# First layer of the first tile by halves of the contraction, with tiny matmuls ahead, in a fused attention and ReGLU kernel

## The chip, the cores and the metric

The kernel runs on one core of a Trainium2 chip. The metric is the device time of one execution in microseconds, taken as the median of several runs; smaller is better. The core has a matrix engine (TensorE, written PE, whose weight loads are listed apart as PEld), a vector engine (VectorE, DVE), a scalar engine (ScalarE, ACT), GpSimd (POOL) and SyncE (SP). Each works through its own queue of instructions in order and waits where a semaphore tells it to. Matmuls write to PSUM, which has eight banks here. POOL and SP also issue DMA transfers.

## The reference

```python
scores = scale * np.matmul(q, k.transpose(0, 1, 3, 2))      # q, k, v: 8 x 8 x 576 x 64
mask = (rel >= 0) & (rel < 64)                              # causal, a window of 64
attn = softmax(np.where(mask, scores, -1e9))
x = np.matmul(attn, v).transpose(0, 2, 1, 3).reshape(4608, 512)
out = (np.maximum(x @ w_gate, 0.0) * (x @ w_val)) @ w_out   # 512 -> 1536 -> 512
```

Inputs and the output are 32-bit floats; the kernel computes in 16-bit floats with 32-bit sums.

## The kernel before, in words

**Two parts in one stream.** Attention is cut into units of 192 query rows (`U`), all eight heads: three units for each of the eight batches. The layers behind it work on tiles of tokens: four tiles of 384 (`TT`, two units each), then six of 512. Tiles 0 and 1 run the plain layers `hidden` and `output`; later tiles run a form with fewer products (`fast_hidden`, matmuls on L634), and the last ones one with seven products for the second layer (`SevenOut`, `SevenLast`, matmuls on L847, with an order of products by name in the table `SEVEN`).

**Who does what.** For a unit: `qk_load` brings q or k of one half of the heads on POOL's DMA queue into `nats` (L179), `qk_trans` transposes it on DVE (L199), `u_st` computes scores on PE (L265, 48 matmuls), `u_exp` takes exponentials on ACT (L299), `u_mask` multiplies by the band on DVE (L306), `u_pv` multiplies by v on PE (L336, 48 matmuls for each half of the heads), `u_recip` (L350) and `u_norm` (L357) normalise on DVE, `u_turn` (L379) transposes into the tile `xt`. v arrives by `v_load` (POOL's queue, L205) and is copied to other partitions by `v_spread`, by DMAs on SP's queue (L217) or, where a copying engine is named, by that engine (L215). `behind_masks` (L312) puts tiny copies on POOL behind a unit's masks. Weight sums (L528) on POOL and DVE prepare the later tiles.

**First layer.** For each of 12 blocks of 128 columns (`f`), `hidden` multiplies the tile by `wg` into one bank and by `wv` into another, four matmuls each over the contraction of 512 (`c` = 0 to 3). ACT applies the ReLU to the first (L572), DVE multiplies it with the second (the gate, L575). In tile 0 the blocks go in pieces of four; the first piece goes by units, in spans of 192 tokens with two blocks in a bank. The weights come in three pieces of 512 columns for each of `wg` and `wv` (`G3`, `V3`), each piece in two DMAs by halves of the contraction (`w_load`, L159), so `c` = 0, 1 can land before `c` = 2, 3. `output` (L1023) is the second layer: out of `g_sb`, with `wo`; ACT copies a bank out (L1035), SP stores it (L1036).

**Banks.** Banks 0 to 3 go round by `one_bank`, banks 4 to 7 in pairs by `two_banks` (scores and pv).

**What sets the order.** The kernel writes all engines' queues in one pass. An object `W` keeps a planned clock. The first and second layers write their matmuls in a fixed order and move the clock by their planned length; every other step has a planned time (`W.at(time, step)`) and is written where the clock passes it. `w_need` moves the clock to the planned landing of a weight piece. The planned times only decide the order in which instructions stand in their queues; in the run each waits only for its data and its place. `plan_batch` gives the planned times of a batch's four q and k loads and of its four transposes; `pair(t, TA, TB, P)` plans the scores of a tile's two units at `TA` and `TB`, and pv, norms and turns from `P` on.

**The start.** PE begins with `u_bias`: eight matmuls (L232) write the band's bias into all banks. `keep_hot` (L229) and `heat` (L226) are matmuls on zeros with no use for the result.

Of the kernel before, what the change touches and what calls it, by code (L numbers as in the profile page):

```python
# [47 lines left out]
def kernel(  # L48
# [10 lines left out]
    nc = tc.nc  # L59
# [4 lines left out]
    U = 192  # L64
    UB = S // U
    NU = B * UB
    NC = DM // 128
    NF = DF // 128
# [85 lines left out]
    def w_load(wt, src, f0, f1, landed):  # L154

        if wt is not wo:
            ns = slice(128 * f0, 128 * f1)
            for a in range(2):
                nc.gpsimd.dma_start(wt[:, 2 * a:2 * a + 2, ns], src.rearrange("(a p e) n -> a p e n", a=2, e=2)[a, :, :, ns])  # L159
        if wt is wo:  # L160
            nc.gpsimd.dma_start(wo[:, f0:f1], src.rearrange("(c p) n -> p c n", p=128)[:, f0:f1])
        w_done.update(((wt.name, f), landed) for f in range(f0, f1))

    def w_need(wt, f):
        while (wt.name, f) not in w_done:
            W.pop()
        W.advance(w_done[wt.name, f])

# [17 lines left out]
    def first_round(name, copies):  # L188
        n = S // 32 * D // len(copies)
        to = nat[0, name, 0] = nats[:, 2 * "kq".index(name)]  # L190
        for i, copy in enumerate(copies):
            copy(to[:, n * i:n * i + n], nat["32", name][:, n * i:n * i + n])
# [30 lines left out]
    def heat(n, to, start=True):  # L223

        for _ in range(n):
            nc.tensor.matmul(to, zero[:, 0:128], zero[:, 0:to.shape[1]], start=start, stop=start, skip_group_check=not start)  # L226

    def keep_hot(to):
        nc.tensor.matmul(to, zero32[:, 0:128], zero32[:, 0:to.shape[1]], start=False, stop=False, skip_group_check=True)  # L229
# [6 lines left out]
    def one_bank():  # L236
        taken["one"] += 1
        to = singles[(taken["one"] - 1) % 4]
        while id(to) in unread:
            W.pop()  # L240
        return to
# [41 lines left out]
    def u_st(u, hhs=(0, 1)):  # L283
        d = units.setdefault(u, {})
        if "st" not in d:
            st_tiles(u)
        run_rows([[st_block(d["st"][g][:, U * hh + 64 * w:U * hh + 64 * w + 64], g, hh, UB * u + w, "biased" in d)
                   for hh in hhs for w in range(UB)] for g in range(G)])
        return 0.29 * len(hhs)
# [117 lines left out]
    def part_written(banks):  # L407
        written.update((id(to), 0) for to in banks)
# [135 lines left out]
    def plan_values(T, u):  # L544
        W.at(T, lambda: u_pv(u))
        W.at(T + 0.6, lambda: u_recip(u))
        for hh in range(2):
            W.at(T + 0.8 + 0.5 * hh, lambda hh=hh: u_norm(u, hh))
        W.at(T + 1.8, lambda: u_turn(u))
# [4 lines left out]
        while normed[0] < n:  # L554
            W.pop()

    def hidden(t, spans, f0=0, f1=NF, each=1):

        if t not in gs:
            gs[t] = g_sb_p.tile([128, NF, WT], FP16, name="g_sb"), {}  # L560
        g_sb, done = gs[t]
        xt = xt_tile(t)
        n = spans[0][1] - spans[0][0]

        w = 512 // n
        each = max(each, w)

        def part(tile):
            return tile[:, 0:w * n].rearrange("p (w n) -> p w n", w=w)

        def relu(r_sb, h1):
            nc.scalar.activation(part(r_sb), part(h1), ACT.Relu)  # L572

        def gate(f, c0, r_sb, h2):
            nc.vector.tensor_tensor(g_sb[:, f:f + w, c0:c0 + n], part(r_sb), part(h2), MUL)  # L575
            done.update(dict.fromkeys(range(f, f + w), c0 + n))

        for fb in range(f0, f1, each):
            r2s = [f_sb.tile([128, 2, WT], FP32, name="pr", bufs=4) for _ in range(2)]
            r_sbs = {}  # L580
            for i, wt in enumerate((wg, wv)):
                for c0, f in ((c0, f) for c0, _ in spans for f in range(fb, fb + each, w)):
                    h = one_bank()
                    part_written([h])
                    for b in range(w):
                        W.advance(W.clock)
                        w_need(wt, f + b)
                        for c in range(NC):
                            nc.tensor.matmul(h[:, b * n:b * n + n], wt[:, c, (f + b) * 128:(f + b) * 128 + 128],  # L589
                                             xt[:, c, c0:c0 + n], start=(c == 0), stop=(c == NC - 1))  # L590
                        W.clock += 4 * (n + 7) / 2400.0
                    if i == 0:
                        r_sb = r_sbs[c0, f] = r2s[len(r_sbs) // 2][:, len(r_sbs) % 2]
                        W.at(W.clock, lambda r_sb=r_sb, h=h: relu(r_sb, h))
                    else:
                        W.at(W.clock, lambda f=f, c0=c0, r_sb=r_sbs[c0, f], h=h: gate(f, c0, r_sb, h))

    def fast_hidden(t, seven=None):

# [467 lines left out]
    XAT = -0.3  # L1067
    SEVEN_LAST = (("P6", "P5", "P2", "P7", "oP1", "P3", "P4"), ("P6", "P5", "P2", "P7", "oP1", "P4", "P3"))
    SEVEN = {n: ("P2", "v0", "v1", "P6", "P5a", "P7", "s0", "P5b", "P4", "s1", "P3") for n in (-5, -4, -3, -2)}
    SEVEN[-1] = ("v0", "P2", "P6", "v1", "P5a", "P7", "P5b", "P4", "h1", "P3")  # L1070

    SEVEN[0] = ("P2", "P4", "P5", "P6", "P7", "P3")

    with tc.manual_schedule():
# [21 lines left out]
        k_zeros()  # L1096
        band_bias()

        first_round("k", (dve, act))
        u_bias(0)  # L1100
        u_bias(1)
# [28 lines left out]
        u_norm(1, 0)  # L1130
        for hh in range(2):
            u_turn(1, (hh,))
        w_load(*G3[1], 20.3)
        w_load(*V3[1], 22.8)
        v_load(2)
        w_load(*G3[2], 27.0)
        w_load(*V3[2], 29.6)
        W.at(23.2, lambda: u_st(2))
        plan_exps(23.2, 2)
        plan_values(27.4, 2)  # L1140

        v_spread(2, pool)
        for name in "kq":
            for hh in range(2):
                qk_load(1, name, hh)
# [3 lines left out]
        for u in (4, 5):  # L1149
            v_load(u)  # L1150
        for i, (name, hh) in enumerate((n, hh) for n in "kq" for hh in range(2)):
            W.at(31.6 + 1.4 * i, lambda name=name, hh=hh: qk_trans(1, name, hh))
        for hh, T in enumerate((36.6, 38.8)):
            W.at(T, lambda hh=hh: u_st(3, (hh,)))
            for i in range(G):
                W.at(T + 0.4 + 0.22 * i, lambda hh=hh, i=i: u_exp(3, i, (hh,)))
                W.at(T + 0.8 + 0.22 * i, lambda hh=hh, i=i: u_mask(3, i, (hh,)))
            W.at(T + 3.5 - 0.7 * hh, lambda hh=hh: u_pv(3, (hh,)))
            W.at(T + 4.0 - 0.7 * hh, lambda hh=hh: u_recip(3, (hh,)))
            W.at(T + 4.1 - 0.7 * hh, lambda hh=hh: u_norm(3, hh))  # L1160
            W.at(T + 4.6 - 0.7 * hh, lambda hh=hh: u_turn(3, (hh,)))
        W.at(37.4, lambda: v_spread(3, pool))
        W.at(40.6, lambda: behind_masks(3))

        def pair(t, TA, TB, P):
            for u, T in ((2 * t, TA), (2 * t + 1, TB)):
# [10 lines left out]
            W.at(T + 1.9, lambda: u_turn(u))  # L1177
            return took

        plan_batch(2, (36.5, 36.6, 42.5, 42.6), (52.0, 53.6, 56.9, 57.1))  # L1180
        plan_batch(3, 58.0, None)
        W.at(58.0, lambda: v_load(8))
        for u in (6, 7):
# [1 line left out]
            W.at(58.0, lambda u=u: v_spread(u))  # L1185
        for u in (4, 5):
            W.at(45.6, lambda u=u: v_spread(u))
        pair(2, 46.6, 50.0, 54.0)
        W.at(52.7, lambda: behind_masks(5))
        pair(3, 62.6, 65.3, None)  # L1190
        W.at(68.0, lambda: behind_masks(7))
# [28 lines left out]
        def ahead(t):  # L1220
            T = W.clock
            long = widths[t] == WT
            ends = T + (32.7 if long else 22.5)
            if t + 2 <= LAST:
                qk_turns(t + 2, T, LATE if t - 1 in FAST_OUT else (0.1, 1.4, 8.0, 14.2) if long else (0.1, 1.4, 6.1, 10.7) if t < NS - 1 else (2.4, 6.1, 10.7, 14.2))
                v_ahead(t + 2, ends, ends + VAT if t in FAST_OUT else ends - 5.0 if long else T + 3.0 if t == 2 else ends + 1.5)
                if t + 1 == NS:
                    W.at(ends + 1.4, lambda: behind_quad(3))
            if t == NS - 2:
                W.at(ends - 0.9, lambda: behind_quad(0, 0))  # L1230
            if t + 3 <= LAST:
                qk_loads(t + 3, (ends - 0.89, ends - 0.88, ends - 0.87, ends - 0.86) if t == NS - 2 else (ends - 15.0, ends - 14.9, ends - 3.0, ends - 2.9) if t < NS else ends - QAT)

        sums = {w: [(w, j, n) for j in range(NF // 4) for n in (0, 1, 3, 2)] for w in (0, 1)}
        for T, gap, eng, some in ((40.5, 0.1, nc.gpsimd, sums[0][:4] + sums[1][:3]), (52.8, 0.1, nc.gpsimd, sums[1][3:8]),
                                  (48.2, 0.6, nc.vector, sums[0][4:8]), (68.1, 0.1, nc.gpsimd, sums[0][8:]),
                                  (64.5, 0.7, nc.vector, sums[1][8:])):
            for i, (w, j, n) in enumerate(some):
                W.at(T + gap * i, lambda eng=eng, w=w, j=j, n=n: w_form(eng, (wg, wv)[w], n, j))
# [9 lines left out]
                pass  # L1249

        W.advance(15.3)
        hidden(0, ((0, U), (U, TT)), 0, 4, 4)
        hidden(0, ((0, TT),), 4, NF, 4)
        hidden(1, ((0, U),), each=4)
        output(0, (0, 1), (0, 8, NF))
        ready(1)
        hidden(1, ((U, TT),), each=4)
        output(0, (2,))
        output(1)
        W.advance(W.clock)  # L1260
        while any(id(one) in unread for one in singles[:4]):
# [73 lines left out]
```

## Time and profile before

| | |
|---|---|
| median of three runs | 301.92 us (301.90 to 302.04) |
| profiled execution | 302.04 us |
| its span, first to last instruction | 300.3 us |
| granted TensorE clock, mean | 1.000 |
| PE busy | 289.6 us, 96% |
| DVE busy | 251.7 us, 84% |
| POOL busy | 201.7 us, 67% |
| ACT busy | 196.0 us, 65% |
| DMA moved | 33.20 MB, mean 111 GB/s |

The profile is one execution, recorded by the hardware. Busy shares are averages over the span; what a wait costs has to be read at its place. In a row of a timeline the first number is the start in us from the span's start, the second the length of the group, then engine, line, operation, output<-input, size, count, and in brackets the idle time before it with what ended it. Landings of loads are told by the time from issue to landing.

### The profile page before, as it was taken

The numbers are of one execution on the slowest core, as the hardware profiler recorded it, in microseconds if no ns is written. First come the engines' busy times: TensorE is split into PE (matmuls) and PEld (weight loads), VectorE is DVE, ScalarE is ACT, GpSimd is POOL, SyncE is SP. The second block draws the span as 40 slices with busy tenths as digits, with TensorE's granted clock in tenths as the row PEclk, the third lists the DMA queues.
The fourth block names the chain that finished last, engine by engine and source line by source line (L and its number), as shares of the span: only waits on it lengthen the run. The fifth ranks groups of instructions, "written<-read, shape, count | busy, mean of one in ns | idle before, by whom it ended". The sixth has DMA issues, their size and how long they took to land.

```text
span 300.3 us, 11073 instructions
## 1 busy us (share of the span) xinstructions
PE 289.6 (96%) x4643; PEld 239.4 (80%) x4643; DVE 251.7 (84%) x517; ACT 196.0 (65%) x408; POOL 201.7 (67%) x241
## 2 busy tenths in 40 slices
PE   4899999999999999999999999999999999999994
PEld 2475877748957975888888888888888888888894
DVE  5947895997995999789999899989858985896584
ACT  3545336258848848885798579857985698538850
POOL 8767689868957893985957595759375617441750
PEclk9999999999999999999999999999999999999999
DMA  7999999979919636911399239922911210031013
GB/s 216 183 196 194 194 197 179 160 131 241 80 40 181 164 70 149 146 42 38 61 219 120 60 53 219 126 57 53 173 37 35 74 41 0 3 103 41 0 38 105
DMA packets 59506, 33.20 MB, mean 111 GB/s; under 512 B 39552, under 2 KB 53824, under 8 KB 59456
## 3 DMA queue, kind: packets, MB, share of 16 engines
q0 software_dynamic: 46688, 18.29, 52.3%
q1 hardware_dynamic: 12192, 13.75, 15.1%
q8 instruction: 36, 0.59, 0.8%
q10 hardware_dynamic: 576, 0.46, 0.5%
q14 instruction: 14, 0.11, 0.1%
HBM read 37.75 MB, written 9.44 MB: 157 GB/s over the span
## 4 chain that ended last, share of the span: by engine, by line
PE 87%; DMA 5%; POOL 4%; DVE 2%; issue 1%; DVEq 0%; POOLq 0%
PE bank L634 46%; PE bank L847 17%; PE bank L589 7%; PE bank L767 5%; PE bank L1023 5%; PE bank L265 3%; DMA wg<-in_moe_w_gate_dram 3%; PE bank L465 2%; DMA v<-in_v_dram 2%; POOL v L205 1%; PE bank L336 1%; POOL wg L159 1%; DVE g_sb L659 1%; DVE g_sb L797 0%; POOL wv L159 0%
## 5 line engine op out<-in xcount | busy, mean ns | idle before, releaser
L659 POOL TENSOR_TENSOR g_sb<-pr 128x512 f16<-128x512 f32 (+1 forms) x36 | 42.7, 1193 | 43.6 <-ACT pr L676 43.6
L670 DVE TENSOR_TENSOR pr<-bank,pr 128x512 f32<-128x512 f32 (+1 forms) x96 | 58.5, 649 | 3.6 <-PE bank L634 1.9
L653 ACT COPY pr<-bank 128x512 f32<-128x512 f32 (+1 forms) x96 | 49.1, 566 | 13.7 <-PE bank L634 13.5
L659 DVE TENSOR_TENSOR g_sb<-r,bank 128x512 f16<-128x512 f32 (+1 forms) x48 | 31.3, 652 | 23.8 <-ACT r L703 22.4
L847 PEld LDWEIGHTS <-g_sb 128*128 128x128 f16 x444 | 41.8, 98 | 5.2 <-issue 0.2
L634 PE MATMUL bank<-xc,vs 128*128 128x256 f16 (+1 forms) x288 | 41.3, 266 | 0.0
L634 PE MATMUL bank<-xc,us 128*128 128x256 f16 (+1 forms) x288 | 41.3, 266 | 0.0
L634 PEld LDWEIGHTS <-vs 128*128 128x128 f16 x384 | 36.5, 98 | 3.5
L634 PEld LDWEIGHTS <-us 128*128 128x128 f16 x384 | 36.5, 98 | 3.3
L205 POOL DMA_DIRECT2D v<-in_v_dram x41 | 34.7, 866 | 2.2 <-DMA nats<-in_q_dram 1.0
L676 ACT ACTIVATE pr<-pr 128x512 f32<-128x512 f32 (+1 forms) x48 | 29.3, 610 | 9.8 <-DVE pr L670 9.8
L703 ACT ACTIVATE r<-bank 128x512 f32<-128x512 f32 (+1 forms) x48 | 27.7, 577 | 4.8 <-PE bank L634 4.0
L634 PEld LDWEIGHTS <-wg 128*128 128x128 f16 x288 | 27.4, 98 | 3.2
L634 PEld LDWEIGHTS <-wv 128*128 128x128 f16 x288 | 27.4, 98 | 2.6
L634 PE MATMUL bank<-xt,wg 128*128 128x256 f16 (+1 forms) x192 | 27.5, 266 | 0.0
L634 PE MATMUL bank<-xt,wv 128*128 128x256 f16 (+1 forms) x192 | 27.5, 266 | 0.0
L797 POOL TENSOR_TENSOR g_sb<-g_sb,xus 128x512 f16<-128x512 f16 x24 | 27.1, 1148 | 0.0
L847 PE MATMUL bank<-wo,g_sb 128*128 128x256 f16 (+1 forms) x222 | 26.6, 270 | 0.0
L430 ACT ACTIVATE pw<-bank 128x512 f16<-128x512 f32 x48 | 25.3, 605 | 1.1 <-PE bank L265 0.7
L847 PE MATMUL bank<-wts,g_sb 128*128 128x256 f16 (+1 forms) x222 | 25.4, 270 | 0.2 <-DVE xw L484 0.2
L643 ACT COPY bank<-bank 128x512 f32<-128x512 f32 (+1 forms) x48 | 24.6, 553 | 0.0
L572 ACT ACTIVATE pr<-bank 128x384 f32<-128x384 f32 x24 | 11.9, 501 | 15.5 <-PE bank L589 12.5
(107 smaller groups left out, 559.8 us busy)
## 6 DMA issues: line engine op xcount, KB each, us to landing
out_dram<-o_sb SPq DMA_DIRECT2D x30, 256.0 KB, 3.1
nats<-in_k_dram POOLq DMA_DIRECT2D x15, 288.0 KB, 6.1
nats<-in_q_dram POOLq DMA_DIRECT2D x15, 288.0 KB, 8.0
v<-in_v_dram POOLq DMA_DIRECT2D x31, 128.0 KB, 8.2
v<-v SPq DMA_DIRECT2D x27, 66.0 KB, 2.7
v<-v SPq DMA_DIRECT2D x13, 132.0 KB, 2.5
wg<-in_moe_w_gate_dram POOLq DMA_DIRECT2D x6, 256.0 KB, 6.4
wv<-in_moe_w_val_dram POOLq DMA_DIRECT2D x6, 256.0 KB, 8.1
```

Source lines behind the costliest of these rows:

```text
L205: nc.gpsimd.dma_start(v16s[b % 2][lo:hi, g, :, 0:64], v[b, :, 64 * g - 64 + lo:64 * g - 64 + hi].rearrange("h p d -> p h d"))
L430: nc.scalar.activation(d["p"][g].rearrange("p n c -> p (n c)"), d["st"][g], ACT.Exp, scale=scale)
L589: nc.tensor.matmul(h[:, b * n:b * n + n], wt[:, c, (f + b) * 128:(f + b) * 128 + 128], xt[:, c, c0:c0 + n], start=(c == 0), stop=(c == NC ...
L634: nc.tensor.matmul(to[:, HT * m:HT * m + HT], w[:, k, 128 * m:128 * m + 128], x[:, k], start=(first and m == 0 and k == 0), stop=(k == 1), ...
L643: nc.scalar.copy(at[j, "B", i][:, 0:TW], at[j, "A", i][:, 0:TW])
L653: nc.scalar.copy(pr[:, i], at[j, "A", i][:, 0:TW])
L659: eng.tensor_tensor(gh[:, f:f + 2, h], pair(r), pair(v), MUL)
L670: nc.vector.tensor_tensor(pr[:, i], to[:, 0:TW], pr[:, i], ADD)
L676: nc.scalar.activation(pr[:, 0], pr[:, 0], ACT.Relu)
L703: nc.scalar.activation(r, to[:, 0:TW], ACT.Relu)
L797: eng.tensor_tensor(to, x, y, op)
L847: nc.tensor.matmul(at[key][:, QN * m * whole:QN * m * whole + n1 - n0], A[:, 128 * m:128 * m + 128], B[:, c, n0:n1], start=(first and m == ...
```

## The change

Seven groups of edits:

- **Halves.** `hidden` gets `halves` and `banks`. With `halves` the banks are taken in groups (for `wg` of the first piece two, otherwise four); first all banks of the group get `c` = 0, 1, then all get `c` = 2, 3. Both calls for tile 0 use it. `w_need` knows the halves of a piece; the first half's planned landing is 1.3 earlier.
- **Tiny matmuls.** 112 matmuls of 4x4 on zeros stand ahead of the bias matmuls, into the bank of the first of them.
- **Second loads.** The planned landings of the second weight pieces move by 1.3; unit 2's `v_spread` is written behind the third pieces' loads, and its values are planned 0.2 later.
- **Second tile.** The k and q transposes of the next batch, unit 3's steps, the copies behind its masks and the weight sums on POOL are planned later, by 0.2 to 1.7. `hidden(1, ...)` for the first unit names its banks.
- **Output of tile 0.** All three blocks of 128 tokens run in one `output` call; before, the third stood behind the second tile's second half.
- **Third tile.** One k transpose 0.7 earlier in the plan, pv of units 4 and 5 1.7 later, and the v loads of tile 4 3.5 later.
- **Last tile.** The product `P7` goes ahead of `P5`, which is no longer split in `P5a` and `P5b`.

```diff
-        w_done.update(((wt.name, f), landed) for f in range(f0, f1))
+        w_done.update(((wt.name, f, a), landed - 1.3 * (1 - a)) for f in range(f0, f1) for a in range(2))
...
-            nc.tensor.matmul(to, zero[:, 0:128], zero[:, 0:to.shape[1]], start=start, stop=start, skip_group_check=not start)
+            nc.tensor.matmul(to, zero[:, 0:to.shape[0]], zero[:, 0:to.shape[1]], start=start, stop=start, skip_group_check=not start)
...
-    def hidden(t, spans, f0=0, f1=NF, each=1):
+    def hidden(t, spans, f0=0, f1=NF, each=1, halves=False, banks=None):
...
+                items = [[(c0, f) for f in range(fb, fb + each, w)] for c0, _ in spans]
+                if halves and i == 1:
+                    items = [sum(items, [])]
+                for group in items if halves else [[item] for items_ in items for item in items_]:
+                    hs = [singles[banks.pop(0)] if banks else one_bank() for _ in group]
+                    part_written(hs)
+                    for cs in ((0, 1), (2, 3)) if halves else (range(NC),):
+                        for (c0, f), h in zip(group, hs):
+                            for b in range(w):
+                                W.advance(W.clock)
+                                w_need(wt, f + b, cs[-1] // 2)
+                                for c in cs:
+                                    nc.tensor.matmul(h[:, b * n:b * n + n], wt[:, c, (f + b) * 128:(f + b) * 128 + 128],
+                                                     xt[:, c, c0:c0 + n], start=(c == 0 and not (halves and b)), stop=(c == NC - 1),
+                                                     skip_group_check=halves)
...
-    SEVEN[-1] = ("v0", "P2", "P6", "v1", "P5a", "P7", "P5b", "P4", "h1", "P3")
+    SEVEN[-1] = ("v0", "P2", "P6", "v1", "P7", "P5", "P4", "h1", "P3")
...
+        heat(112, units[0]["st"][0][0:4, 0:4])
         first_round("k", (dve, act))
...
-        w_load(*G3[1], 20.3)
-        w_load(*V3[1], 22.8)
+        w_load(*G3[1], 21.6)
+        w_load(*V3[1], 24.1)
         v_load(2)
         w_load(*G3[2], 27.0)
         w_load(*V3[2], 29.6)
+        v_spread(2, pool)
         W.at(23.2, lambda: u_st(2))
         plan_exps(23.2, 2)
-        plan_values(27.4, 2)
-
-        v_spread(2, pool)
+        plan_values(27.6, 2)
...
-            W.at(31.6 + 1.4 * i, lambda name=name, hh=hh: qk_trans(1, name, hh))
-        for hh, T in enumerate((36.6, 38.8)):
+            W.at((32.0, 33.4, 34.8, 36.2)[i], lambda name=name, hh=hh: qk_trans(1, name, hh))
+        for hh, T in enumerate((37.6, 39.8)):
...
-            W.at(T + 3.5 - 0.7 * hh, lambda hh=hh: u_pv(3, (hh,)))
+            W.at(T + 3.5, lambda hh=hh: u_pv(3, (hh,)))
...
-        W.at(40.6, lambda: behind_masks(3))
+        W.at(41.6, lambda: behind_masks(3))
...
-        plan_batch(2, (36.5, 36.6, 42.5, 42.6), (52.0, 53.6, 56.9, 57.1))
+        plan_batch(2, (36.5, 36.6, 42.5, 42.6), (52.0, 52.9, 56.9, 57.1))
...
-        pair(2, 46.6, 50.0, 54.0)
+        pair(2, 46.6, 50.0, 55.7)
...
-                v_ahead(t + 2, ends, ends + VAT if t in FAST_OUT else ends - 5.0 if long else T + 3.0 if t == 2 else ends + 1.5)
+                v_ahead(t + 2, ends, ends + VAT if t in FAST_OUT else ends - 5.0 if long else T + 6.5 if t == 2 else ends + 1.5)
...
-        for T, gap, eng, some in ((40.5, 0.1, nc.gpsimd, sums[0][:4] + sums[1][:3]), (52.8, 0.1, nc.gpsimd, sums[1][3:8]),
+        for T, gap, eng, some in ((41.5, 0.1, nc.gpsimd, sums[0][:4] + sums[1][:3]), (52.8, 0.1, nc.gpsimd, sums[1][3:8]),
...
-        hidden(0, ((0, U), (U, TT)), 0, 4, 4)
-        hidden(0, ((0, TT),), 4, NF, 4)
-        hidden(1, ((0, U),), each=4)
-        output(0, (0, 1), (0, 8, NF))
+        hidden(0, ((0, U), (U, TT)), 0, 4, 4, True)
+        hidden(0, ((0, TT),), 4, NF, 4, True)
+        hidden(1, ((0, U),), each=4, banks=[0, 1, 4, 5, 2, 3, 0, 1, 2, 3, 0, 1])
+        taken["one"] += 2
+        output(0, (0, 1, 2), (0, 4, 8, NF))
         ready(1)
         hidden(1, ((U, TT),), each=4)
-        output(0, (2,))
         output(1)
```

More of the change, by code (lines that the diff above doesn't have):

```diff
@@ L161, in w_load, with w_need @@
             nc.gpsimd.dma_start(wo[:, f0:f1], src.rearrange("(c p) n -> p c n", p=128)[:, f0:f1])
-        w_done.update(((wt.name, f), landed) for f in range(f0, f1))
-    def w_need(wt, f):
-        while (wt.name, f) not in w_done:
+        w_done.update(((wt.name, f, a), landed - 1.3 * (1 - a)) for f in range(f0, f1) for a in range(2))
+    def w_need(wt, f, a=1):
+        while (wt.name, f, a) not in w_done:
             W.pop()
-        W.advance(w_done[wt.name, f])
+        W.advance(w_done[wt.name, f, a])
     nat = {}
@@ L581, in hidden @@
             for i, wt in enumerate((wg, wv)):
[L582 to L596, printed above, removed]
+                items = [[(c0, f) for f in range(fb, fb + each, w)] for c0, _ in spans]
@@ new lines, in hidden @@
+                if halves and i == 1:
[12 more added lines that the diff above has]
+                                                     skip_group_check=halves)
+                                W.clock += len(cs) * (n + 7) / 2400.0
+                            if cs[-1] < NC - 1:
+                                continue
+                            if i == 0:
+                                r_sb = r_sbs[c0, f] = r2s[len(r_sbs) // 2][:, len(r_sbs) % 2]
+                                W.at(W.clock, lambda r_sb=r_sb, h=h: relu(r_sb, h))
+                            else:
+                                W.at(W.clock, lambda f=f, c0=c0, r_sb=r_sbs[c0, f], h=h: gate(f, c0, r_sb, h))
@@ L1157 @@
                 W.at(T + 0.8 + 0.22 * i, lambda hh=hh, i=i: u_mask(3, i, (hh,)))
-            W.at(T + 3.5 - 0.7 * hh, lambda hh=hh: u_pv(3, (hh,)))
-            W.at(T + 4.0 - 0.7 * hh, lambda hh=hh: u_recip(3, (hh,)))
-            W.at(T + 4.1 - 0.7 * hh, lambda hh=hh: u_norm(3, hh))
-            W.at(T + 4.6 - 0.7 * hh, lambda hh=hh: u_turn(3, (hh,)))
+            W.at(T + 3.5, lambda hh=hh: u_pv(3, (hh,)))
+            W.at(T + 4.0, lambda hh=hh: u_recip(3, (hh,)))
+            W.at(T + 4.1, lambda hh=hh: u_norm(3, hh))
+            W.at(T + 4.6, lambda hh=hh: u_turn(3, (hh,)))
         W.at(37.4, lambda: v_spread(3, pool))
-        W.at(40.6, lambda: behind_masks(3))
+        W.at(41.6, lambda: behind_masks(3))
         def pair(t, TA, TB, P):
```

## The prediction

> **What bounds the kernel now.** I read the page first: engine shares, slices, chain by engine.
>
> ```profile
> PE 289.6 (96%) x4643; PEld 239.4 (80%) x4643; DVE 251.7 (84%) x517; ACT 196.0 (65%) x408; POOL 201.7 (67%) x241
> ...
> PEclk9999999999999999999999999999999999999999
> ...
> PE 87%; DMA 5%; POOL 4%; DVE 2%; issue 1%; DVEq 0%; POOLq 0%
> ```
>
> TensorE is busy for 96% of a span of 300.3 us and carries 87% of the chain. So a change pays only where PE stands still, and the list of what PE waits for says where:
>
> ```profile
> PE bank L232 <- DVE bias L129: 4.4, 1, 4.4
> PE bank L589 <- DMA wg<-in_moe_w_gate_dram: 0.7, 2, 0.4
> PE bank L589 <- DVE xt L379: 0.7, 1, 0.7
> PE bank L265 <- DVE qT L199: 0.5, 1, 0.5
> ...
> PE bank L847 <- DVE xw L484: 0.2, 1, 0.2
> ```
>
> Then PE's timeline from 11 to 31 us, where the change works (start, length, operation, count, idle before):
>
> ```profile
> 14.51 1.33 PE L589 MATMUL bank<-xt,wg 128*128 128x192 f16 x14 [0.35 <-DMA wg<-in_moe_w_gate_dram]
> 16.50 1.48 PE L589 MATMUL bank<-xt,wg 128*128 128x192 f16 x16 [0.66 <-DVE xt L379]
> 17.82 2.80 PE L589 MATMUL bank<-xt,wv 128*128 128x192 f16 x32
> ...
> 26.24 0.49 PE L589 MATMUL bank<-xt,wg 128*128 128x384 f16 x2
> 27.09 0.50 PE L589 MATMUL bank<-xt,wg 128*128 128x384 f16 x2 [0.36 <-DMA wg<-in_moe_w_gate_dram]
> ```
>
> Between 17.82 and 26.24 PE works without a hole. At 26.24 two matmuls of the third gate piece run, and the next two wait for its second contraction half. At 162.5 ns from start to start they were due at 26.24 + 2 x 0.1625 = 26.57, so 27.09 is 0.52 late. The windows view gives PE 12.13 busy of 13.50 us from 13.6 to 27.1, and 41.90 of 41.90 from 27.1 to 69: no hole at all for 42 us. Whatever PE gains before 27 has to get through a stretch that has no idle time now only because DVE and the loads arrive just in time.
>
> **First tile by halves.** The matmul count stays. Three things shift. (a) The 0.52 us at 27.09 goes: both halves of the contraction are separate passes over four banks, so after the first half's landing there are 8 matmuls (1.3 us) and the third unit's 48 pv matmuls (0.5 us) ahead of the first matmul that needs the second half. (b) The second unit's first passes need only the first turn (13.22 plus 1.03 for two, and 14.95 plus 0.58 = 15.53). The row at 16.50 waited for the last turn (15.80 + 0.58 = 16.38). By halves, its first 8 matmuls (8 x 0.0825 = 0.66 us) run before 16.38. So the wv pass begins at 16.50 + 0.66 = 17.16 instead of 17.82, a lead of 0.66. (c) It costs something: four banks now finish in the second pass 0.325 apart (two 128x384 matmuls), but DVE's gate multiply frees them 0.47 apart (27.20 1.00 for two). The next piece reuses those banks and waits for each: the first finished bank is free at once, the others lag 0.145 each, at most 3 x 0.145 = 0.44. It is met at two piece ends. Before the third piece there is also the landing of the first half: it stays at about 25.78 (the row at 26.24 is its first user), so the lead of (b) can't pass that point whole. I take the lead behind the first tile, on the matmul stream of before, as 0.5 us: the 0.52 removed, with (b) used up by (c) and that landing. Bounds: 0.66 (the lead of (b) survives whole) and, below nothing, -0.36 (both piece ends lose 0.44 and (b) never comes: 0.52 - 0.88).
>
> **Tiny matmuls.** 112 matmuls of 4x4 on zeros run while PE waits anyway for the bias (4.41). They need only the zeros that DVE fills (2.05 plus 0.38 = 2.43). No row has such a size. Nearest from below: 48 scores matmuls of 32x64 last 0.55 us in four groups side by side, 12 in a group: about 30 ns each in a group. From above: 128x192 at 82.5 ns. I take 30: 112 x 0.03 = 3.4 us, done at 5.8. The bias matmuls took 0.32 each while the rows were slow and would take 0.1625 at the later rate: 1.3 us, then 0.91 for the FP32 matmuls of L229, ending at 8.0. The first scores start at 8.38, held by DVE's transposes (7.07 + 1.26 = 8.33). Cost 0. If the cover goes, PE's idle spells up to 14.51 (0.23, 0.46, 0.23, 0.35: 1.27 us in the timeline) still absorb a delay; 82.5 ns would give 9.2 us, a delay of about 5.5 and a loss of some 4.2.
>
> The Trainium skill, "TensorE: Matmul & The Clock Gate", Part 1 ("Wait — 56ns, not 53.3ns?"), gives small matmuls a floor of about 25 ns, and about 62 ns each where the sequencer's microcode issues them. By the first the cost is 0; by the second 112 x 0.062 = 6.9 us, with the rival below. No row here separates the two.
>
> **Third unit and the second tile.** The third unit's scores keep their place in PE's order (between wg and wv of the second piece); the masks go ahead of the gates on DVE, four of 0.35: no PE wait, since PE's next user of those four banks is the gate-paced one costed in (c). Its v copies are written earlier in the text and stand in the same place in POOL's order: nothing. The pieces' later planned landings move no load, only the plan. The second tile's use of banks 4 and 5 for wv takes banks that no one holds then: nothing. The fourth unit's scores come later: the program's order has 20 first-layer matmuls (1.65 us) more ahead of the first half. Less the lead, its masks come about 0.4 to 0.9 later; DVE, busy without a hole from 31.3 to 45.2, has two more gates (0.93) ahead of them, less 0.5: 0.43. POOL's tiny copies behind these masks (42.15) hold six weight sums of 1.16 us and then the q loads of the third batch, issued at 49.69 and 50.26. So those two may be issued up to 0.4 later.
>
> **The crossing at 63 us.** Units 4 and 5's pv move later, and on DVE the two q transposes now stand behind the first of the four norms; before, they stood behind three. DVE's timeline, and the issues of SP and POOL and PE's scores from theirs:
>
> ```profile
> 57.06 1.02 DVE L357 TENSOR_TENSOR xus<-bank,r 128x384 f16<-128x384 f32 x2
> 58.00 1.03 DVE L379 STREAM_TRANSPOSE xt<-xus 128x384 f16<-128x384 f16 x2
> ...
> 60.00 2.31 DVE L199 STREAM_TRANSPOSE qT<-nats 128x576 f32<-128x576 f32 x2
> 62.16 0.54 DVE L357 TENSOR_TENSOR xus<-bank,r 128x384 f16<-128x384 f32 x1
> ```
>
> ```profile
> 49.34 1.16 SPq L1036 DMA_DIRECT2D out_dram<-o_sb  x2
> ```
>
> ```profile
> 49.69 1.11 POOL L179 DMA_DIRECT2D nats<-in_q_dram  x2
> ```
>
> ```profile
> 63.03 0.55 PE L265 MATMUL bank<-qT,kT 32*128 32x64 f16 x48
> ```
>
> The trace has the two q landings at 57.51 and 59.25 (7.8 and 9.0 us after issue). Unit 6's scores need all four score banks, so the last norm. From the second landing: transpose 1.08, norm 0.47, two turns 0.95, two reciprocals 0.16, norm 0.46, gate 0.46, norm 0.55, and 0.1 to PE: 4.23 us, so 63.48. In PE's order 20 instead of 23 512-wide matmuls are left behind the scores, so without any wait they would come at 63.03 + 3 x 0.216 = 63.68 less the lead of 0.5, 63.18. With the landing as it is PE stalls 0.3 and keeps 0.2 of its lead. With the loads 0.2 later (half of 0.4) the scores start at 63.68, and the lead is gone. The size of the lead hardly matters then: the landing sets the time. I take the middle, 63.58, a gain of 0.1.
>
> The third store of tile 0 (256 KB) goes out with the other two around 50 instead of at 63.79, on SP's queue behind the second, which landed at 58.58. It competes with the loads for the last stretch; I take 0 since the second store alone already kept that queue occupied until 0.7 us before the landing. Bound: its share of a landing 1.05 us later (60.3). The v loads that move behind one gate product on POOL (1193 ns in the mean) are for two tiles later, and a tile takes 24 us (the chain's L634 pieces start at 69.24 and 93.62): nothing.
>
> **The late product order.** P7 takes its place before P5 in the last tile. In before, PE stood from the end of the pv at 263.2 to 263.59 (0.18 named, 0.37 with the usual switch of 0.12) until DVE had read the banks that P5 writes. P7 writes others: gain 0.25.
>
> ```profile
> 263.59 2.67 PE L847 MATMUL bank<-wts,g_sb 128*128 128x256 f16 x23 [0.18 <-DVE xw L484]
> ```
>
> **Sum.** -0.1 at 63 us, -0.25 at 263: -0.35 on the profiled run of 302.04 (span 300.3 and 1.74 around it): 301.69. That run lies 0.12 above the median of 301.92, so 301.6 against the median. A change of less than 0.2% (0.6 us) can't be told here from none.
>
> **Rivals.**
> - *No stall at 63.* If the q loads land by 58.9, or PE's pv comes so that DVE's chain is not held by them, the whole lead of 0.5 arrives, at best 0.65: 301.92 - 0.5 - 0.25 = 301.2. For it: if PE and POOL run 0.5 earlier, so do the issues, and the engines' busy shares in the DMA view from 45 to 66 us fall to four to seven tenths at about 52 to 53. Against: they are nine tenths or more from there to 59. Chance 0.30.
> - *The landing moves out, slower.* One mechanism: the early third store, and POOL's later issue, push the second q landing. It decides from 60.3 on: scores at 60.3 + 4.23 = 64.53 against 63.68, less 0.25, is +0.6; at 60.4, +0.7: 302.6. For it: the latency of 9 us with queues full. Against: the third store sits behind the second. Chance 0.18.
> - *Sequencer-bound tiny matmuls.* At t ns each the scores begin at 2.45 + 112t + 2.2; the idle spells absorb until 45 ns. At 56 ns: 10.9 against 8.38, less 1.27, is +1.3: 302.9. Chance 0.06. By the skill's 62 ns it would be +1.95.
> - *The halves don't shift anything.* If the second unit still starts at 16.50 and the gates take the 0.52 back, the lead is 0, but so is the stall: 63.68 stands, -0.25 stays: 301.7. Chance 0.08.
>
> **Numbers.** Forecast 0.38 (own range 301.2 to 302.2; about 0.05 of it falls beyond the bound as faster). Faster 0.30 + 0.05 = 0.35; same 0.33 + 0.08 = 0.41; slower 0.18 + 0.06 = 0.24. The range takes in the no-stall case with 0.65 of lead (301.0) and the moved landing at its price and 0.1 more (302.7); it leaves out the tiny matmuls' rival and tails.
>
> **What would show it.** In the profile after: no wait for the wg load at the third piece; short waits of PE on the gates of L575 at the piece ends; first scores still near 8.4; PE's wait before unit 6's scores near 63, with a norm as releaser, and the qT transposes waiting for the nats load on DVE; no wait of P5 near 263. A PE wait before 8.4 that ends later, a second q landing beyond 60.3, or no stall at 63 would make the forecast wrong.

## Result and profile after

The kernel after takes 305.25 us in the median of six runs (304.61 to 306.66) against 301.92 before: a ratio of 1.0118, interval 1.0089 to 1.0146. It is 3.3 us slower; the forecast was 301.6, and its range ended at 302.7. The profiled run is the longest of the six, 306.66 us with a span of 305.0, so its waits add up to more than the median lost.

The page of the kernel after, engines and chain, and the instruction queue's line:

```profile
PE 294.0 (96%) x4755; PEld 242.0 (79%) x4755; DVE 252.3 (83%) x517; ACT 195.4 (64%) x408; POOL 201.4 (66%) x241
...
q8 instruction: 37, 0.61, 0.8%
...
PE 91%; DMA 3%; DVE 2%; issue 1%; ACT 1%; POOL 0%; DVEq 0%; ACTq 0%; POOLq 0%
```

Shares hardly move (PE 96% in both), so the page alone says little. What PE waited for says more (total, times, longest):

```profile
PE bank L226 <- DVE wts L1096: 2.5, 1, 2.5
PE bank L336 <- issue: 1.4, 1, 1.4
PE bank L855 <- issue: 0.9, 2, 0.7
PE bank L465 <- issue: 0.6, 1, 0.6
PE bank L265 <- DVE qT L199: 0.5, 1, 0.5
PE bank L594 <- DVE xt L379: 0.3, 1, 0.3
PE bank L594 <- DVE g_sb L575: 0.2, 1, 0.2
```

The wait for the `wg` load is gone. New are four waits put down to "issue": PE stood with nothing that the profile shows to wait for. They are 1.4 to 0.3 us long and lie in or just behind streams of pv matmuls. The start in the kernel before, for comparison:

```profile
4.41 2.72 PE L232 MATMUL bank<-bias,ident 128*128 128x384 f16 x8 [4.41 <-DVE bias L129]
...
8.38 0.55 PE L265 MATMUL bank<-qT,kT 32*128 32x64 f16 x48
```

And after, the start, an end of a piece, and the largest of the four waits:

```profile
2.48 2.94 PE L226 MATMUL bank<-wts 128*4 128x4 f16 x112 [2.48 <-DVE wts L1096]
5.36 2.74 PE L232 MATMUL bank<-bias,ident 128*128 128x384 f16 x8
7.89 1.49 PE L229 MATMUL bank<-wts 128*128 128x384 f32 x2
9.31 0.73 PE L265 MATMUL bank<-qT,kT 32*128 32x64 f16 x48
...
27.41 0.48 PE L594 MATMUL bank<-xt,wg 128*128 128x384 f16 x2
28.14 1.41 PE L594 MATMUL bank<-xt,wg 128*128 128x384 f16 x6 [0.25 <-DVE g_sb L575]
```

```profile
58.11 0.64 PE L336 MATMUL bank<-v,p 128*32 128x65 f16 x56
60.13 0.49 PE L336 MATMUL bank<-v,p 128*32 128x65 f16 x40 [1.38 <-issue]
```

The first scores start at 9.31 instead of 8.38. The bias matmuls are 0.32 us apart as before, although PE had worked for 2.9 us ahead of them. Near 27 the wait changed its releaser: the gates of DVE instead of the load. At 58 a stream of 96 pv matmuls is cut in two.

**What ends the holes.** In the trace, each of the four ends 1.36 to 1.47 us behind the end of a packet of queue q8. That queue moves packets of 16,384 bytes: 37 in this run, 36 in the one of before. The page counts 2 x 4755 = 9510 matmuls and weight loads of PE, and 2 x 4643 = 9286 before. That fits one packet for 256 instructions of 64 bytes (9510/256 = 37.1, 9286/256 = 36.3). Now count PE's records in order from the first weight load on: weight loads, matmuls and the few semaphore instructions between them, one each. The first instruction behind a hole then has a number that is 192 modulo 256, in each of the long holes of these traces that no data explains. (The expectations below count a little otherwise and say 181 to 183.) A hole is given here from the start of the last matmul ahead of it to the start of the next; t40, t168 and b112 are runs of the next section.

| kernel (tiny matmuls) | hole, us | number of the first instruction behind it | packet ended | hole ends after that |
|---|---|---|---|---|
| before (0) | 15.60 to 16.50 | 448 = 256 + 192 | 15.04 | 1.46 |
| after (112) | 58.55 to 60.13 | 1984 = 7 x 256 + 192 | 58.72 | 1.41 |
| after (112) | 143.15 to 143.91 | 4800 = 18 x 256 + 192 | 142.45 | 1.47 |
| after (112) | 205.38 to 205.94 | 6848 = 26 x 256 + 192 | 204.52 | 1.42 |
| after (112) | 236.53 to 237.45 | 7872 = 30 x 256 + 192 | 236.09 | 1.36 |
| t40 (40) | 63.31 to 64.66 | 1984 | 63.28 | 1.38 |
| t168 (168) | 63.77 to 65.27 | 2240 = 8 x 256 + 192 | 64.00 | 1.27 |
| b112 (112) | 57.28 to 60.13 | 1984 | 58.79 | 1.34 |

In all 16 traces PE passes no such boundary earlier than 1.25 us behind the end of its packet. So these are waits for instructions. PE has its program in blocks of 256; where a block falls onto fast streams (96 pv matmuls, 192 instructions, take 1.1 us), PE is through before the next block is there. The tiny matmuls put 224 instructions ahead of everything, and all later boundaries fall 224 places earlier in the work. The Trainium skill, "Runtime: NRT & Kernel Launch", section "Instruction fetch mechanics", says that instructions come in blocks of 16 KiB, 256 of them, and that crossing a boundary is mostly hidden. The blocks agree with the packets here; "mostly hidden" does not hold for this kernel, in which PE stood for up to 2.85 us at one boundary (57.28 to 60.13 in b112). Why the place is 192 and not 0 is open.

The first row is from the kernel before, and there the two causes can't be told apart: the prediction read that hole, as the profile labels it, as a wait for the last turn (16.38), which was there 0.1 earlier. In the run of the last tile's order alone, whose front is that of before, the turn was done at 16.37, and PE went on at 17.30, 1.43 behind its packet.

### The profile page after: what moved, and what is told of

It reads as the page before. It is cut to its first block, busy times and chain, and to the rows that moved or that the text cites. A ratio compares the mean times of both kernels' runs of the same rounds, so it can differ in the third digit from the quotient of the medians.

```text
span 305.0 us, 11301 instructions
## 1 busy us (share of the span) xinstructions
PE 294.0 (96%) x4755; PEld 242.0 (79%) x4755; DVE 252.3 (83%) x517; ACT 195.4 (64%) x408; POOL 201.4 (66%) x241
## 4 chain that ended last, share of the span: by engine, by line
PE 91%; DMA 3%; DVE 2%; issue 1%; ACT 1%; POOL 0%; DVEq 0%; ACTq 0%; POOLq 0%
PE bank L642 45%; PE bank L855 18%; PE bank L594 9%; PE bank L775 5%; PE bank L1031 5%; PE bank L265 3%; DMA nats<-in_q_dram 3%; PE bank L465 2%; PE bank L336 2%; DVE p L306 1%; DVE qT L199 0%; ACT pr L572 0%; DVE xt L379 0%; DVE g_sb L575 0%; PE bank L229 0%
## 5 line engine op out<-in xcount | busy, mean ns | idle before, releaser
L711 ACT ACTIVATE r<-bank 128x512 f32<-128x512 f32 (+1 forms) x48 | 27.7, 577 | 5.1 <-PE bank L642 4.4
L572 ACT ACTIVATE pr<-bank 128x384 f32<-128x384 f32 x24 | 11.0, 496 | 18.2 <-PE bank L594 15.4
```

Of the source, the lines that this page charges most:

```text
L711: nc.scalar.activation(r, to[:, 0:TW], ACT.Relu)
```

## The experiments

Each kernel was run beside the kernel before and is compared with those runs. In the experiments on tiny matmuls, theory A is that PE runs out of instructions. Its rival: the tiny matmuls cost only their own time.

**Count of tiny matmuls, in the kernel after.** With n = 0, 40, 128, 168 (and 96 below):

```diff
-        heat(112, units[0]["st"][0][0:4, 0:4])
+        heat(n, units[0]["st"][0][0:4, 0:4])
```

n = 0:

> The kernel after without the 112 tiny matmuls (224 fewer PE instructions). In the profile after PE stood four times for 0.5 to 1.6 us with no releaser, each time at an instruction whose number is 181 to 183 modulo 256 and each time 1.36 to 1.47 us behind the end of a 16 KB packet of the instruction queue (q8). Theory A (PE runs out of instructions where a block of 256 falls onto fast pv streams; the tiny matmuls shifted the block boundaries by 224): the four stalls move or shrink, the first scores start near 8.4 instead of 9.3, and the time is 301.5 to 302.5. Theory B (the tiny matmuls cost their own time at the start, 0.9 to 1.1 us, and the rest of the loss is the retimed steps behind): 304 to 304.5, with the later holes still there.

n = 128:

> The kernel after with 128 tiny matmuls instead of 112: 256 instructions, exactly one block, ahead of everything, so the block boundaries behind lie as with none. Theory A: the later holes of the kernel without tiny matmuls, and its time plus what the start costs (first scores at about 9.3 + 16 x 0.026 = 9.7, so about 1.4 later): 302.5 to 304. Theory B: a little slower than with 112, 305.3 to 306, with the same holes behind.

n = 40:

> The kernel after with 40 tiny matmuls: 1.0 us from 2.48, done before the bias is there (4.4), so the start costs nothing. By the order of PE's instructions no block of 256 then falls on less than 3.7 us of PE work behind 30 us (with none, the shortest are 1.6 to 3.0; with 112, 1.3 to 2.3). Theory A: no hole without a releaser behind 20 us, and 0.2 to 1.0 faster than with none: 301.0 to 301.8. Theory B: as with none.

n = 168:

> The kernel after with 168 tiny matmuls: the start is held until 2.48 + 168 x 0.026 = 6.9 and the first scores come near 10.8, but the block boundaries lie as with 40 (one block more). Theory A: no hole behind 20 us; the time is that with 40 plus the late start of up to 2.4: 302.5 to 304, faster than with 112 although it runs 56 more. Theory B: slower than with 112 by another 1.4: 306.5 or more.

Measured, with 301.65 for before: 302.58 for 0 (ratio 1.0026, 1.0015 to 1.0036; just above A's range), 303.62 for 128 (1.0070, 1.0054 to 1.0087), 304.15 for 40 (1.0084, 1.0071 to 1.0098), 306.94 for 168 (1.0169, 1.0156 to 1.0183). By their own time they can't be ordered so: 128 is faster than 112 and than 40. The 40 matmuls end at 3.62, before the bias is there at 4.42, and still cost 1.6 us. The waits of PE with 40 and with 128:

```profile
PE bank L336 <- issue: 1.8, 1, 1.8
PE bank L1031 <- issue: 1.0, 1, 1.0
```

```profile
PE bank L226 <- DVE wts L1096: 2.5, 1, 2.5
PE bank L594 <- DVE xt L379: 1.5, 1, 1.5
```

With 0 and 128, whose boundaries coincide, PE has one hole, at the second unit's first matmul (448 and 704); with 40 and 168, which also coincide, it has two, in the second pv stream (15.27 with 40) and near 64. The expectation for 40 and 168 was wrong: only blocks shorter than 3.7 us behind 30 us were counted as short. Near 64 us (in the run with 40) a block of 4.0 us of work was too short: the packet for the next began only 2.9 us behind the crossing of the boundary before it, and the next block could start 2.4 later still. Behind 140 us, with little other traffic, packets started up to 1.3 us ahead of the crossing in the run without tiny matmuls, and its blocks of 1.8 to 2.6 us did no harm. So the theory told where holes can be, but not how long a block must be: that hangs on when the queue's packet gets through.

The profiled runs allow a closer look, matmul by matmul against the one without tiny matmuls. With 128, PE is a steady 0.8 us late from 24 us to the end. With 112 it is 0.5 late at 35 us, gains 1.5, 0.7, 0.5 and 0.8 at the four holes, and ends 4.0 late.

**96 in the kernel after.**

> The kernel after with 96 tiny matmuls instead of 112. Instruction numbers at the block boundaries move by 32. By the order of PE's instructions the first two blocks are fetched as early as with 112 (PE crosses the first boundary within the tiny matmuls, near 5 us), and the short blocks behind 130 us become 2.9 to 3.7 us of work instead of 1.3 to 2.3. Near 53 us a block of 5.3 us stays, where with 112 a fetch needed 7.3 from the crossing. Theory A (instruction supply): the holes behind 130 us gone, the one near 55 to 60 stays or grows, first scores 0.4 earlier than with 112: 303 to 304.5. Theory B (the count of tiny matmuls alone): as with 112 less 0.4, 304.8, with the holes.

Measured 304.69 (1.0083, 1.0065 to 1.0102), just above A's range and just under B's 304.8; the time does not decide. The trace does: the hole near 59 stays (58.94 to 60.23, number 1984), those of 143, 205 and 237 are gone, and one of 0.5 is at 240.6, number 8128, again 192 modulo 256. Position again goes by the number.

**Tiny matmuls alone, in the kernel before.** The same line with 112, and later with 128:

```diff
+        heat(112, units[0]["st"][0][0:4, 0:4])
         first_round("k", (dve, act))
```

> The kernel before with the 112 tiny matmuls alone. Theory A (instruction supply): by the order of PE's instructions the blocks that start near 139, 170, 200 and 230 us become 1.3, 1.7, 2.1 and 2.5 us of work (3.0 to 1.7 without), so holes with no releaser of up to 1 us at instruction numbers of 181 to 183 modulo 256 show behind 130 us; the hole or wait at the second unit's first layer (16.5) moves away from the block boundary; first scores near 9.3: 303 to 304.5. Theory B (the start alone): 302.5 to 302.9, no holes behind 130.

> The kernel before with 128 tiny matmuls, 16 more than in the run with 112 (307.49): exactly one block of 256 instructions ahead, so the block boundaries fall where they fall in the kernel before. Theory A (instruction supply): the holes with no releaser behind 40 us are gone, only the late start is left, about 1.0 as between none and 128 in the kernel after: 303.0 to 303.8, so 4 us faster than with 16 fewer. Theory B (the tiny matmuls' own time): 307.9.

Measured 307.49 with 112 (1.0180, 1.0163 to 1.0197; before at 302.17), 303.12 with 128 (1.0038, 1.0026 to 1.0050; before at 301.91). Sixteen more matmuls, 0.4 us of PE work, make the kernel 4.4 us faster (4.1, each against its own runs of before). The pv stream of units 4 and 5 with 112, and then with 128:

```profile
56.72 0.75 PE L336 MATMUL bank<-v,p 128*32 128x65 f16 x64
60.13 0.42 PE L336 MATMUL bank<-v,p 128*32 128x65 f16 x32 [2.66 <-issue]
```

```profile
55.41 1.06 PE L336 MATMUL bank<-v,p 128*32 128x65 f16 x96
```

The rival, the tiny matmuls' own time, falls with this. It is a part: 128 against none, with equal boundaries, costs 1.0 us in the kernel after (303.62 to 302.58) and 1.2 in the one before.

Not all of the loss with 112 is the holes themselves. The profiled run is the longest of its six (310.33), and in it the granted TensorE clock is 0.50 from 60.90 to 64.30, 0.8 us behind the long hole; the 16 wv matmuls there last 2.77 instead of 1.48. PE is 5.0 us late just ahead of that stretch and 6.6 behind it. The first row is of the windows view, with the clock third from the end:

```profile
60.90:64.30 3.40, 3.40 (x23) 3.07 (x21) 1.31 (x4) 0.49 (x1) 2.94 (x4) 0.50 0.50 78
```

```profile
61.41 2.77 PE L589 MATMUL bank<-xt,wv 128*128 128x192 f16 x16
```

The profiled run with 40 has such a stretch too (16.03 to 19.44, behind the hole that ends at 15.27), and shorter waits, of 1.0 us, stand ahead of one near 13 in b112 and one near 12 with 96. But those with 128 and 168 have none behind holes of 1.7 us, and the one of the kernel after has none. What brings it is open. The comparison of 112 and 128 does not hang on it: the three runs with 112 whose mean granted clock was 0.998 or more took 305.93 to 307.39, against 302.93 to 303.56 with 128.

**The halves alone.** Kernel before with the new `hidden` and both calls for tile 0 by halves:

```diff
-        hidden(0, ((0, U), (U, TT)), 0, 4, 4)
-        hidden(0, ((0, TT),), 4, NF, 4)
+        hidden(0, ((0, U), (U, TT)), 0, 4, 4, True)
+        hidden(0, ((0, TT),), 4, NF, 4, True)
```

> The kernel before with the halves alone (both calls for tile 0), nothing else. Without tiny matmuls the kernel after kept PE waits on DVE's gate multiply at both piece ends: 0.28 before the second piece, 0.52 before the third (rows at 21.5 to 28.6 us), which is as much as the 0.52 us wait for the weights that the halves took away, plus 0.28. Theory A (banks that finish 0.325 apart are freed 0.465 apart by DVE): slower than before by 0.2 to 0.4 us, the wait for the wg load gone. Theory B (the loss of that kernel against before, 0.9 us, came from the retimed steps behind, not from the halves): faster by 0.3 to 0.5.

Measured 303.49 against 301.95 (1.0051, 1.0031 to 1.0072): slower by more than expected. PE waits on gates before the second piece (0.14 twice, over the usual distance of two matmuls), the third (0.28 and twice 0.14), and once in the second tile (0.65 at 34.67). The second unit's start at 17.03 instead of 16.50 (1.59 behind its packet) adds to the loss in this trace.

**Halves for `wg` alone.**

```diff
             for i, wt in enumerate((wg, wv)):
+                hv = halves and i == 0
...
-                if halves and i == 1:
-                    items = [sum(items, [])]
-                for group in items if halves else [[item] for items_ in items for item in items_]:
+                for group in items if hv else [[item] for items_ in items for item in items_]:
...
-                    for cs in ((0, 1), (2, 3)) if halves else (range(NC),):
+                    for cs in ((0, 1), (2, 3)) if hv else (range(NC),):
```

> The kernel before with halves for wg alone; wv keeps one bank after the other, so its banks finish 0.65 apart and the gates (0.465 each) keep up. Theory A: no waits on gates at the piece ends, the wait for the third wg piece gone: faster than before by 0.3 to 0.5 us, unless a wait near 63 us takes it back. Theory B: the same as with halves for both.

Measured 302.51 (1.0016, 1.0006 to 1.0025): neither. The waits at the second piece are gone, but PE still waits 0.61 near 27 for a gate. DVE's timeline of this kernel shows why:

```profile
25.30 0.94 DVE L306 TENSOR_TENSOR p<-p,mask 128x384 f16<-128x384 f16 x2
26.17 0.54 DVE L575 TENSOR_TENSOR g_sb<-pr,bank 128x384 f16<-128x384 f32 x1
26.63 0.61 DVE L306 TENSOR_TENSOR p<-p,mask 128x384 f16<-128x384 f16 x2
27.17 1.01 DVE L575 TENSOR_TENSOR g_sb<-pr,bank 128x384 f16<-128x384 f32 x2
```

The third unit's masks stand between the gates, and the third bank is read only at 27.7. In the kernel before DVE's queue stood in the same order (gates at 26.20 and 27.20 behind masks); it did not show, because PE was held by the load at that time.

**Masks behind the gates.** The same with

```diff
-        plan_exps(23.2, 2)
-        plan_values(27.4, 2)
+        plan_exps(23.2, 2, mask=False)
+        for i in range(G):
+            W.at(27.0 + 0.01 * i, lambda i=i: u_mask(2, i))
+        plan_values(28.3, 2)
```

> The kernel before with halves for wg alone, and unit 2's four masks behind the four gates of the second piece on DVE (before: between them), its pv after two more banks. With halves for wg alone PE still waited 0.61 near 27 for a gate that stood behind those masks. Theory A (DVE's queue was behind the weights' wait): both waits near 27 go, faster than before by 0.2 to 0.5 unless a later wait takes it; the second unit's start at 16.4 to 17.3 varies with the instruction fetch. Theory B: another wait of the same size near 27 to 30.

Measured 301.94 against 302.17 (0.9995, 0.9986 to 1.0004): both waits near 27 are gone, and PE runs through:

```profile
26.50 2.11 PE L593 MATMUL bank<-xt,wg 128*128 128x384 f16 x12
28.55 0.56 PE L336 MATMUL bank<-v,p 128*32 128x65 f16 x48
```

Of the 0.5 us little arrives at the end: the second unit's start at 16.76 (1.49 behind its packet) takes 0.26 of it in this run, and tile 2 starts at 69.07, as before (69.08). The expected gain of 0.2 to 0.5 is not shown.

**The last tile's order alone.**

> The kernel before with the last tile's order of products alone (P7 before P5). The prediction said 0.25 us faster: PE's 0.37 before P5a goes. In the kernel after without tiny matmuls PE waits 0.24 at that place for ACT's copy of P6 instead. Theory A: 0.1 to 0.15 faster, with that ACT wait. Theory B: 0.25.

The edit is the line of `SEVEN[-1]`. Measured 301.73 against 301.95 (0.9988, 0.9974 to 1.0002), which can't be told from nothing by itself. In the trace PE's spell at 263 is 0.24 above the usual distance instead of 0.37, and ACT's copy ends it: 0.13 gained.

**Retimed steps without halves and tiny matmuls**, that is, the kernel after with `heat` and both `True` taken out:

> The kernel after without the tiny matmuls and without the halves: the retimed steps, the early third store and the last tile's order remain. With the halves this kernel was 0.9 us slower than before; the halves alone cost 1.5. Theory A (the halves' gate waits are what the front loses): 301.3 to 302.0, within 0.2% of before, PE's wait for the third wg piece back near 27, no PE wait of over 0.3 at unit 6's scores near 63. Theory B (the retimed steps or the third store cost something of their own): 302.5 or more, with a wait near 63.

Measured 303.82 against 302.17 (1.0053, 1.0041 to 1.0066): theory A fell. The loss isn't near 63 but at two waits on gates in the second tile's second half, 54.53 to 55.72 and 60.03 to 61.05.

**The kernel after without tiny matmuls, with the halves mended** (for `wg` alone, masks behind the gates as above):

> The kernel after without tiny matmuls, with halves for wg alone and unit 2's masks behind the gates. On the kernel before, this form of the halves took PE's waits near 27 us away (301.94 against 302.17). Theory A (the retimed steps behind are good for a stream that has no waits on gates): 301.0 to 301.8, no PE wait of over 0.3 from 18 to 69 us. Theory B (the retimed steps fit only the planned clock of the halves as they are, as they cost 1.6 without halves): 302.5 or more, with PE waits on gates of L575 near 55 or 61.

Measured 303.50 against 301.91 (1.0050, 1.0037 to 1.0062): theory B. PE waits on gates until 55.42 (0.49 over the usual distance) and until 56.98 (0.90). DVE's timeline of this kernel has a k transpose in front of the second:

```profile
54.83 0.54 DVE L575 TENSOR_TENSOR g_sb<-pr,bank 128x384 f16<-128x384 f32 x1
55.30 1.24 DVE L199 STREAM_TRANSPOSE kT<-nats 128x576 f32<-128x576 f32 x1
56.38 1.00 DVE L575 TENSOR_TENSOR g_sb<-pr,bank 128x384 f16<-128x384 f32 x2
```

In the kernel after without tiny matmuls alone, where the halves move the second tile's matmuls to another place of the plan, PE shows no wait on gates there.

**Both that helped**: kernel before, halves for `wg` alone, masks behind the gates, and the last tile's order:

> The kernel before with halves for wg alone, the masks behind the gates and the last tile's order of products. Theory A: 0.3 to 0.7 faster than before, 301.2 to 301.6. Theory B: as before.

Measured 301.62 against 302.17 (0.9988, 0.9979 to 0.9997): a little faster than the kernel before, by 0.36 us (0.0012 x 302.17), at the low end of what was expected.

## Why the prediction was wrong

**Tiny matmuls, "Cost 0": the step that failed.** They cost 2.7 us (305.25 less 302.58), the bulk of 3.3. Their length was taken too long, 30 ns against 2.94 us / 112 = 26 ns; the rival of 56 or 62 ns each was wrong. The Trainium skill, "TensorE: Matmul & The Clock Gate", section "Wait — 56ns, not 53.3ns?", gives a floor of about 25 ns, and the trace's 26 agrees. Two terms of the sum failed. The bias matmuls were put at 0.1625 and stayed at 0.32, L229 took 1.49 instead of 0.91, so the first scores came at 9.31 instead of below 8.38. That start is about 1 us (the run with 128 against none; 0.5 in the profiled run with 112). The larger rest, about 1.7, is the instruction queue, which the prediction did not think of: it counted what 112 matmuls take, not that 224 instructions shift every block boundary behind them. The label "issue" was not in the waits of before, and the one hole there was of that kind was labelled as a turn.

**First tile by halves: the term (c) was mis-sized, and (b) did not arrive.** The load's 0.52 went, as said. In its place stand waits on gates, 0.28 before the second piece and 0.52 before the third (without tiny matmuls), where the step charged the lead of (b) for them and kept 0.5 whole. It took the gates as 0.47 apart and free of other work; DVE had four masks among them. And (b), 0.66 from an earlier start of the second unit, fell to the block boundary at 448: with halves for `wg` alone, the turn that the unit's first passes need was done at 15.52, as the step has it, yet the unit started at 16.76, 1.35 behind the packet. In the kernel after without tiny matmuls tile 1 begins at 33.37 against 32.57, 0.80 later, and so beyond the step's own lower bound of -0.36; 0.51 of it is the second unit's start (17.01).

The 0.52 itself was less than it seemed. In the run of the last tile's order alone the second unit started 0.80 later than in the profile of before; PE then had no wait for the load near 27, and tile 2 began only 0.26 later (69.34). So that wait was there because the second unit had started early in the one profile that was read, and taking it away could not be worth 0.5 us in every run.

**Steps moved.** The k transpose that moves 0.7 earlier was not costed at all. In the kernel with mended halves two gates stand behind it, and PE loses 0.90 there. In the run without halves the transpose at 54.04 is likewise ahead of the gate that PE waits for until 55.72 (1.1 lost). No run moves this step alone, so its share is read from the timelines.

**The crossing at 63 us** was not tested: PE came to unit 6's scores late on its own (66.42 after, 64.47 without tiny matmuls) and showed no wait there. POOL issued the q loads 2.0 later than before, not 0.4, yet the second landed at 60.65, 1.4 later, in 8.4 instead of 9.0 us; without tiny matmuls 1.5 later and landed at 59.19. So a landing near 60 neither came from the early third store nor did it decide. Nor is the 59.25 that the step started from a fixed point: in the run of the last tile's order alone, issued 0.14 earlier, the same load landed at 56.87.

**Late order.** Half the size: 0.13 instead of 0.25, since ACT's copy of P6 is what P7 waits for next.

**What was right**: that PE alone counts, that the lead would not survive the stretch to 69 us, that a gate of DVE takes the place of the load.

Without tiny matmuls the kernel after is 0.26% slower than before; halves, retiming and late order together cost 0.8 us (0.0026 x 301.65). How these divide can't be read from the single runs: the halves alone cost 1.5, the retimed steps alone 1.6, and both together less than either. The halves move the planned clock, and with it the place of the retimed steps in the queues; that this is the whole reason is not shown.

## What to carry to other kernels

Count the instructions that an edit puts on PE's queue, not only their time: where a hole has no releaser, compare its end with the packets of the instruction queue and the instruction's number modulo 256. Before a wait for a load is removed, look at what the engine behind it has done by that time; a queue that is late too will show up in its place. And planned times that were fitted to one order are not an edit of their own: tested alone, they cost as much as the part that they were fitted to.

## What the runs showed of the hardware

- PE's instructions come in packets of 16,384 bytes on queue q8; in the 16 traces a block is never used earlier than 1.25 us behind the end of its packet, and the holes end 1.25 to 1.59 behind it. Where other transfers were dense (11 to 60 us) the packet began up to 5.2 us behind PE's crossing of the boundary one block earlier; from 140 us on it began between 1.6 ahead and 3.1 behind.
- 112 matmuls of 4x4 did not speed up the eight bias matmuls behind them: 0.32 us each with and without.
- In the profiled run of b112 the granted TensorE clock fell to 0.50 for 3.4 us, 0.8 us behind a hole of 2.85; with 168 a hole of 1.7 was not followed by that.
- In the six kernels with 96 or more tiny matmuls the first k load landed at 4.94 to 5.56 us; in the others at 4.55 to 4.80, issued at 0.82 in all. What links the two is open.
